# Attention with two feed-forward layers on one core: the first eight pairs' scores in plain float32 from four landing buffers, PSUM banks held back until a result has room, five buffers for the last outputs

## The chip, the cores and the metric

One NeuronCore of a Trainium2 chip runs the whole program. The metric is device time in microseconds (us) of one execution, lower is better. Five engines work side by side: PE (matrix multiply), DVE (VectorE), ACT (ScalarE), POOL (GpSimd) and SP, which here only issues DMAs.

## The reference

```python
# q, k, v: 4 batches, 8 heads, 576 positions, 64 wide (float32)
scores = scale * np.matmul(q, k.transpose(0, 1, 3, 2))
mask = block_i >= block_j          # blocks of 64 positions
scores = np.where(mask, scores, -1000000000.0)
scores = scores - np.max(scores, axis=-1, keepdims=True)
attn = np.exp(scores)
attn = attn / (np.sum(attn, axis=-1, keepdims=True) + 1e-09)
x = np.matmul(attn, v)             # laid out as 2304 tokens x 512
h = x @ w_in                       # 512 x 1024, softmax-like gate, layer norm with gain g_ln
y = ln @ w_out                     # 1024 x 512
h = y @ w_in2                      # 512 x 2048
out = (h / (1 + np.exp(-1.702 * h))) @ w_out2
```

## The kernel before

**Precision by terms.** A float32 operand is kept as two parts: H, a copy rounded to the type float32r (`qkH`, made by `nc.copy`), and L, the rest (`qkL = x - H`, made by `rest`, line 550). A product is then three matmuls: H with H, H with L, L with H. The probabilities times v (`u_pv`, line 671) are plain float32 matmuls instead, with no splitting; the trace shows each such instruction as two records.

**Pairs.** The 32 heads are worked in 16 pairs of two heads, four pairs to a batch. The two heads lie on partitions 0 to 63 and 64 to 127, so a score matmul of one head uses 64 rows of the array. A pair has an X part (queries 0 to 255: `scores(p, 0)`, `u_pt(p, "X")`, `u_pv(p, "X")`) and a Y part (the other 320 queries: `scores(p, 2)`, `scores(p, 3)`, `scores(p, "R")`, then `u_pt` and `u_pv`). R is the last block of 64 queries of both heads: before, `qR` holds them on the diagonal of a 128x128 tile, so that one matmul of 128 rows serves both heads.

**From scores to output.** `scores` (line 695) writes two PSUM banks; a reduction on DVE adds the mask, writes the result to an SBUF tile `P` and finds the row extreme `mx`; an exponential on ACT rewrites `P` and sums it into `sm`. `u_pt` (line 632) transposes `P` on PE into a bank, and ACT or DVE copies that to `ptx` or `pty`. `u_pv` multiplies by v; the result goes through `xo` to the DRAM tensor `xd`. There are two sets of `P` tiles (p % 2), one `pty` and one `ptx`. `norm` (line 748) ends a half of a batch: reciprocal of the sums `sm`, a transpose on PE (`ident,sm`), `rt` to DRAM. These eight transposes are good landmarks in the trace.

**Loads.** q and k of a pair land in the one buffer `raw_qk` (line 517). `load_qk` (line 602) takes column ranges, `split_qk` (line 619) makes H, L and the `qR` tiles: per pair one copy of 2x576 columns, one subtraction, four copies of 64x64. The X parts of pairs 0 to 3 come first, each from half of `raw_qk`; then the rest of q and k is loaded and split (for pairs 0 and 1 all of k a second time).

**Feed-forward layers.** `w1_prep` (line 586) turns the eight-byte weights of the first layer into float32 and splits them (tiles `e`, `r`, `w1i`, `w1o`). The first layer works on tiles of 128 tokens: `x_take`, `h_mm` (matmuls `w1i,xs`), `solu_ln`, `ln_t`, `y_mm`. The second layer runs after attention is over, its results go through the two buffers `ob` (list `obs`, line 1266) to the output (`out_steps`, line 1211).

**What sets the order.** All this is recorded by a `Recorder` (line 60) with a priority each, `a_time` for attention and `f_time` for the first layer (lines 979 to 1007: `T0` and `F_RATE` set when first-layer work is due, `PREP` when weight preparation is). `issue` (line 349) then writes one fixed program per engine: it takes the work with the earliest modelled start. Banks are handed out there: a group of matmuls that needs a bank gets one as soon as one is free. `_end` (line 336) chooses among engines for a copy and counts the waiting work of an engine up to `SPAN` behind in priority. On the chip each engine runs its list in order and waits on semaphores.

Of the kernel before, what the change touches and what calls it, by code (L numbers as in the profile page):

```python
# [21 lines left out]
def full(t):  # L22
    return t.bitcast(F32)
# [36 lines left out]
class Recorder:  # L60
# [6 lines left out]
    SPAN = 3  # L67
# [4 lines left out]
    def __init__(self, tc, banks):  # L72
        self.banks = banks
        self.n_bank = banks.shape[1]
        self.bank_free = [True] * self.n_bank
        self.bank_t = [0.0] * self.n_bank
        self.n_buf = 0
        self.places = {}

        self.floor = 0.0  # L80
        self.tc = tc
        self.nc = tc.nc
        self.prio = 0.0
        self.tag = None
        self.n_tag = {}
        self.open = None
        self.ops = []
        self.tensors = {}
        self.free = dict.fromkeys(self.ENGINES, 0.0)
        self.port = 0.0  # L90
        self.dma = 0.0
        self.now = 0.0
        self.heap = {e: [] for e in self.ENGINES}
        self.log = []
        for e in self.ENGINES:
            setattr(self, e, _Engine(self, e))
# [114 lines left out]
    def _cost(self, eng, name, kw, outs, ins):  # L211
# [5 lines left out]
        if eng == "tensor":  # L217
            if name == "transpose":
                return 0.109, 0.2, False
            k = kw["lhsT"].shape[0]  # L220
            if kw["lhsT"].dtype == F32:

                return max(0.109, 0.87 * n / 1000), 0.3, False
# [34 lines left out]
    def _add(self, forms):  # L258
# [10 lines left out]
        for eng, calls in forms.items():  # L269
            cost, port, lag = 0.0, False, 0.0  # L270
            for name, args, kw in calls:
# [12 lines left out]
                touched = [(self._place(a), False) for a in ins] + [(self._place(a), True) for a in outs]  # L284
# [137 lines left out]
def kernel(  # L422
# [22 lines left out]
    BLK = 64  # L445
# [21 lines left out]
    y1d = [dram.tile([DM, CH], F32, name=f"y1d{c}") for c in range(NC)]  # L467
    nc = Recorder(tc, psum.tile([128, 8, 512], F32, name="PS"))
# [48 lines left out]
    raw_qk = ap1.tile([128, 2, S], F32, name="rawqk")  # L517
# [84 lines left out]
    def load_qk(p, qs, ks, at):  # L602

        b, i = divmod(p, NPB)
        for n, (x, s) in enumerate(((q, qs), (k, ks))):
            nc.sync.dma_start(out=raw_qk[:, n, s.start + at:s.stop + at], in_=x[b, i, :, s])
# [12 lines left out]
    def split_qk(p, qs, ks, at):  # L619

        for i, s in ((slice(0, 2), qs),) if qs == ks else ((0, qs), (1, ks)):
            H, L = (x[:, i, s] for x in qkb[p % 2])
            r = raw_qk[:, i, s.start + at:s.stop + at]
            nc.copy(H, r)
            rest(L, r, H)
        if qs.stop == S:
            for t, r in zip(qkb[p % 2], qR[p % 2]):
                for h in range(2):
                    d = slice(64 * h, 64 * h + 64)
                    nc.copy(r[d, d], full(t)[d, 0, S - BLK:S])  # L630

    def u_pt(p, what):
# [8 lines left out]
        if two:  # L641
            t2 = nc.bank(1, 2, name="T")
        for blocks, h, i in todo:
            n = len(blocks)
            t = t2[:, h] if two else nc.bank(1, name="T")
# [3 lines left out]
            src = t[:, 0:n * 128]  # L649
            if two:  # L650
                if h == 0:
                    continue
                src = t2[:, :, 0:n * 128]
                h = slice(0, 2)
            pty = ptyb[p % NPTY]
            if what == "R":
                if i:
                    dst = pty[:, :, 3 * NQ:3 * NQ + BLK]
                    src = src.rearrange("p (h s) -> p h s", h=2)
                else:  # L660
                    dst = pty.rearrange("p h (j s) -> p h j s", s=NQ)[:, :, :, QX:NQ]
                    src = src.rearrange("p (j h s) -> p h j s", j=n, h=2)
            elif what == "X":
                dst = ptx[:, h]
            else:
                at = slice(128 * (i - 2), 128 * (i - 1))
                dst = pty.rearrange("p h (j s) -> p h j s", s=NQ)[:, h, 0:i + 1, at]
                src = src.rearrange("p h (j s) -> p h j s" if two else "p (j s) -> p j s", s=128)
            nc.copy(dst, src, "av")
# [25 lines left out]
    def scores(p, what):  # L695
# [5 lines left out]
        (qH, kH), (qL, kL) = ((x[:, 0], x[:, 1]) for x in qkb[p % 2])  # L701
        t = [nc.bank(2, name="S") for _ in range(2)]
        if what == "R":
            H, L = qR[p % 2]
            half = S // 2
            for c in range(2):
                ks = slice(c * half, (c + 1) * half)
                with nc.group():
                    for n, (x, y) in enumerate(((H, kH), (H, kL), (L, kH))):
                        nc.tensor.matmul(t[c][:, 0:half], lhsT=x, rhs=y[:, ks], start=n == 0, stop=n == 2)  # L710
# [6 lines left out]
        else:  # L717
# [3 lines left out]
            with nc.group():  # L721
                for i in ((0, 1) if what == 0 else (what,)):
                    w = 128 * (i + 1)
                    for n, (x, y) in enumerate(((qH, kH), (qH, kL), (qL, kH))):
                        for h in range(2):
# [3 lines left out]
                                start=n == 0, stop=n == 2,  # L729
# [136 lines left out]
    def attention():  # L866
# [20 lines left out]
        def load(p, qs, ks, vt, half=0):  # L887
            yield 0.0, (load_qk, p, qs, ks, QX * half)
            yield 0.0, (load_v, p, vt)

        def split_1(p, qs, ks, vt, half=0):
            yield 0.0, (split_qk, p, qs, ks, QX * half)


        todo = [(p, first, first, vx, p % 2) for p in range(NPB)]
        for p in range(2):
            yield from load(*todo[p])
        yield 0.0, (clear,)
        yield from split_1(*todo[0])
        for p in range(NPB):  # L900
            if p + 1 < NPB:
                yield from split_1(*todo[p + 1])
            if p + 2 < NPB:
                yield from load(*todo[p + 2])
            yield from x_part(p)
        yield 0.0, (norm, 0, 0)
        yield 0.0, (ended, QX)
        turn = list(range(NPB - 2, NPB)) + list(range(NPB - 2))
        todo = [(p, later, later if p >= NPB - 2 else every, vy) for p in turn]
        todo += [(p, every, every, ve) for p in range(NPB, NP)]  # L910

        def take(*a):
            yield from load(*a)
            yield from split_1(*a)

        yield from take(*todo[0])
        yield from take(*todo[1])
        for n, (p, *_) in enumerate(todo):
            both = [(y_part(p, take(*todo[n + 2]) if n + 2 < len(todo) else None), 7.5)]
            if n + 1 < len(todo) and todo[n + 1][0] >= NPB:  # L920
                both.append((x_part(todo[n + 1][0]), 2.0))
# [57 lines left out]
    T0 = 5  # L979
# [3 lines left out]
    F_RATE = 1.6  # L983
    PREP = 3
# [226 lines left out]
    def out_steps(cc, p):  # L1211
# [12 lines left out]
        for i, a in enumerate(acc[cc]):  # L1224
# [5 lines left out]
            if last:  # L1230
                a.buf.held = False
                o = obs[next(n_ob) % len(obs)]
# [119 lines left out]
```

## Time and profile before

| | us |
|---|---|
| median of 3 runs | 798.61 |
| lowest and highest | 798.06, 798.86 |
| profiled execution | 797.17 |
| its span, first to last instruction | 795.4 |

The profiled execution lies 1.44 us under the median, and its span 1.77 us under its own time. In the views a row of the timeline gives start, duration, engine, line, operation and out<-in with the partition and element counts; "x4" is four instructions merged into a row; in brackets stands the idle time before and the instruction that ended it. The ends of matmuls are modelled and overlap with the next start, so a step on PE is best priced from its start to the start of what follows. Almost every instruction carries line 347, where the recorder emits.

### The profile page before, as it was taken

How to read it: one execution, taken by the hardware profiler on the slowest of the kernel's cores; microseconds unless marked ns; L12 is line 12 of the kernel's file. 1: busy time of each engine (PE TensorE's matmuls, PEld its weight loads, DVE VectorE, ACT ScalarE, POOL GpSimd, SP SyncE). 2: the span in 40 equal slices, each digit the busy share in tenths (PEclk: the TensorE clock that was granted, in tenths of full speed). 3: DMA queues.
4: the chain of work that ended last, by engine and by line, in shares of the span. 5: the costliest groups of instructions: out<-in, count | busy, mean ns of one | idle time of the engine just before them, and what ended most of it. 6: DMA issues, size and time to landing. Idle time of an engine off the chain costs nothing.

```text
span 795.4 us, 14078 instructions
## 1 busy us (share of the span) xinstructions
PE 765.7 (96%) x4984; PEld 659.5 (83%) x4984; DVE 555.6 (70%) x1256; ACT 455.7 (57%) x1034; POOL 292.6 (37%) x355
## 2 busy tenths in 40 slices
PE   5898999999999999999999999999999999999996
PEld 3576777888787899898998789898988898989895
DVE  3689877655766487855747987978899765565643
ACT  5798978675856565645634645445575543434431
POOL 2245642361430254632322514324632342353310
PEclk9999999999999999999999999999999999999999
DMA  7654734533421254366411163644525222050201
GB/s 194 201 153 147 224 111 129 155 104 108 124 70 59 93 144 158 108 192 192 144 57 53 55 202 103 190 166 147 187 70 183 79 97 89 28 160 1 68 13 53
DMA packets 82342, 95.63 MB, mean 120 GB/s; under 512 B 11232, under 2 KB 57696, under 8 KB 82272
## 3 DMA queue, kind: packets, MB, share of 16 engines
q1 hardware_dynamic: 82272, 94.74, 38.2%
q8 instruction: 39, 0.64, 0.3%
q14 instruction: 31, 0.25, 0.1%
HBM read 69.47 MB, written 25.24 MB: 119 GB/s over the span
## 4 chain that ended last, share of the span: by engine, by line
PE 80%; DVE 9%; ACT 3%; DMA 3%; issue 2%; POOL 1%; SPq 1%; DVEq 0%; ACTq 0%; POOLq 0%
PE PS L347 80%; DMA e<-in_moe_w_in_dram 1%; SPq L347 1%; DVE sg L347 1%; DVE gL L347 1%; DVE w2oL L347 1%; ACT pty L347 1%; DVE w2SL L347 1%; DVE hc L347 1%; DVE u L347 1%; DVE w1i L347 1%; DVE e L347 1%; DVE qkL L347 1%; DVE st L347 1%; DMA r<-rcd 0%
## 5 line engine op out<-in xcount | busy, mean ns | idle before, releaser
L347 ACT ACTIVATE sg<-hc 128x256 f32<-128x256 f32 (+1 forms) x128 | 56.3, 443 | 108.3 <-DVE hc L347 99.5
L347 PE MATMUL PS<-w2oH,gH 128*128 128x512 f32 x288 | 113.4, 394 | 0.4 <-ACT gH L347 0.4
L347 PE MATMUL PS<-w2oH,gL 128*128 128x512 f32 x288 | 113.5, 394 | 0.2 <-DVE gL L347 0.2
L347 PE MATMUL PS<-w2oL,gH 128*128 128x512 f32 x288 | 113.4, 394 | 0.0
L347 PE MATMUL PS<-lnTH,w1o 128*128 128x256 f32 x576 | 111.2, 285 | 0.0
L347 PE MATMUL PS<-w1i,xs 128*128 128x512 f32 x432 | 108.0, 397 | 0.8 <-ACT pty L347 0.8
L347 PE MATMUL PS<-w1i,w2SH 128*128 128x320 f32 (+1 forms) x512 | 105.7, 296 | 0.2
L347 PEld LDWEIGHTS PS<-lnTH,w1o 128*128 128x128 f32 x576 | 91.1, 188 | 1.6 <-issue 0.6
L347 PEld LDWEIGHTS PS<-w1i,xs 128*128 128x128 f32 x432 | 78.2, 188 | 16.3 <-ACT pty L347 1.0
L347 PEld LDWEIGHTS PS<-w1i,w2SH 128*128 128x128 f32 x512 | 84.4, 189 | 5.0 <-DVE w1i L347 0.5
L347 POOL TENSOR_TENSOR sg<-hc,sg 128x256 f32<-128x256 f32 (+1 forms) x45 | 36.7, 817 | 128.0 <-ACT sg L347 124.1
L347 PE MATMUL PS<-lnTL,w1o 128*128 128x256 f32 x288 | 81.3, 282 | 0.0
L347 ACT ACTIVATE gH<-sg 128x256 fp32r<-128x256 f32 (+1 forms) x122 | 53.1, 442 | 44.2 <-DVE sg L347 29.0
L347 PE MATMUL PS<-w1i,w2SL 128*128 128x320 f32 (+1 forms) x256 | 75.6, 295 | 0.0
L347 ACT ACTIVATE P<-P,mx 128x128 f32<-128x128 f32 (+3 forms) x128 | 70.6, 554 | 7.5 <-DVE mx L347 7.2
L347 DVE CUSTOM_DVE_ANT_0 P<-PS,mask 128x128 f32<-128x128 f32 (+3 forms) x128 | 57.3, 486 | 22.2 <-PE PS L347 18.9
L347 DVE TENSOR_TENSOR hc<-PS,u 128x320 f32<-128x320 f32 (+1 forms) x96 | 42.8, 454 | 40.4 <-PE PS L347 37.4
L347 PEld LDWEIGHTS PS<-w2oH,gL 128*128 128x128 f32 x288 | 54.0, 188 | 13.5 <-DVE gL L347 1.2
L347 PEld LDWEIGHTS PS<-w2oH,gH 128*128 128x128 f32 x288 | 54.1, 188 | 10.3 <-ACT gH L347 1.2
L347 PEld LDWEIGHTS PS<-w2oL,gH 128*128 128x128 f32 x288 | 54.1, 188 | 8.9
L347 DVE TENSOR_TENSOR gL<-sg,gH 128x320 fp32r<-128x320 f32 (+1 forms) x95 | 48.1, 517 | 10.9 <-ACT gH L347 10.1
L347 PEld LDWEIGHTS PS<-lnTL,w1o 128*128 128x128 f32 x288 | 54.3, 189 | 0.7 <-DVE lnTL L347 0.2
(164 smaller groups left out, 1731.6 us busy)
## 6 DMA issues: line engine op xcount, KB each, us to landing
land<-in_moe_w_in_dram SPq DMA_DIRECT2D x16, 512.0 KB, 4.1
land<-in_moe_w_out_dram SPq DMA_DIRECT2D x16, 512.0 KB, 4.2
x<-y1d SPq DMA_DIRECT2D x16, 512.0 KB, 3.8
w2d<-wt SPq DMA_DIRECT2D x24, 256.0 KB, 2.6
wt<-w2d SPq DMA_DIRECT2D x24, 256.0 KB, 2.6
y1d<-yo SPq DMA_DIRECT2D x36, 128.0 KB, 1.7
part<-ob SPq DMA_DIRECT2D x18, 256.0 KB, 3.5
out_dram<-ob SPq DMA_DIRECT2D x18, 256.0 KB, 2.5
```

What stands on the lines that cost most here:

```text
L347: getattr(getattr(self.nc, e), name)(*map(real, args), **{k: real(v) for k, v in kw.items()})
```

## The change

- **Landing buffers.** Three buffers `rawqk0` to `rawqk2` and a piece of `x_all` take the place of the one `raw_qk`; pairs use them in turn as they use the v buffers. q and k of a pair come whole, or for pairs 0 to 3 as first 256 and later 320 columns, nothing twice.
- **Plain float32 scores.** For pairs 0 to 7 (`NFULL`) there is no H, no L and no `qR`: one float32 matmul from the landing buffer takes the place of three. R becomes, per half of the keys, one matmul of 64 rows to 64 partitions for each head, both heads into one bank. Pairs 8 to 15 stay as they were.
- **Banks.** With `also` the destination that the result of a bank will be copied to counts as written by the matmul group itself, so the group, and its bank, waits until that destination is free.
- **First activation.** An exponential on one column (`begun`) is issued at the start.
- **Last outputs.** In the last pass over the last chunk the three tiles `t` join the two `ob`.
- **Numbers.** SPAN 3 to 10, T0 5 to 10, F_RATE 1.6 to 1.4, PREP 3 to 2, and a lag for plain float32 matmuls of 64 rows.

```diff
-    SPAN = 3
+    SPAN = 10
...
-                touched = [(self._place(a), False) for a in ins] + [(self._place(a), True) for a in outs]
+                touched = [(self._place(a), False) for a in ins] + [(self._place(a), True) for a in outs + self.also]
+                self.also = []
...
+    begun = const.tile([128, 1], F32, name="begun")
+    tc.nc.scalar.activation(out=begun, in_=mhalf, func=ACTF.Exp)
...
-    raw_qk = ap1.tile([128, 2, S], F32, name="rawqk")
+    rawb = [ap1.tile([128, 2, S], F32, name=f"rawqk{i}") for i in range(3)]
+    rawb.append(x_all[:, 1024:1024 + 2 * S].rearrange("p (n s) -> p n s", n=2))
+
+    NFULL = 8
...
+    def split_qk(p):
+
+        if p < NFULL:
+            return
+        H, L = qkb[p % 2]
+        r = rawb[vat(p)]
+        nc.copy(H, r)
+        rest(L, r, H)
...
+            if not two or h == 0:
+                nc.also = [dst]
...
+        if p < NFULL:
+            terms = [(rawb[vat(p)][:, 0], rawb[vat(p)][:, 1])]
+        else:
+            (qH, kH), (qL, kL) = ((x[:, 0], x[:, 1]) for x in qkb[p % 2])
+            terms = [(qH, kH), (qH, kL), (qL, kH)]
         t = [nc.bank(2, name="S") for _ in range(2)]
+
+        nc.also = [P[x] for x in (["R"] if what == "R" else [(h, i) for h in range(2) for i in ((0, 1) if what == 0 else (what,))])]
...
+            with nc.group():
+                for c in range(2):
+                    ks = slice(c * half, (c + 1) * half)
+                    for h in range(2) if p < NFULL else ():
+                        d = slice(64 * h, 64 * h + 64)
+                        x, y = terms[0]
+                        nc.tensor.matmul(
+                            t[c][d, 0:half], lhsT=x[d, S - BLK:S], rhs=y[d, ks], start=True, stop=True
+                        )
...
-                    for n, (x, y) in enumerate(((qH, kH), (qH, kL), (qL, kH))):
+                    for n, (x, y) in enumerate(terms):
...
         for p in range(NPB):
+            yield from load(p, first, vx)
+            if p == 0:
+                yield 0.0, (clear,)
+        for p in range(NPB):
             yield from x_part(p)
+            yield from load(p, later, vy)
...
-    T0 = 5
+    T0 = 10
...
-    F_RATE = 1.6
-    PREP = 3
+    F_RATE = 1.4
+    PREP = 2
...
-                o = obs[next(n_ob) % len(obs)]
+
+                at = obs + [x[:, 0:DM] for x in tmpb] if p == NPAIR - 1 and cc == len(chunks) - 1 else obs
+                o = at[next(n_ob) % len(at)]
```

On PE, from pair 1's transposes to the end of pair 2's first scores, the list before stands so (`P` and `ptx` as above, `v` the values, `ident` marks a transpose, numbers are buffers):

```order
L347 MATMUL PS<-ident,P_155 128x128
L347 MATMUL PS<-ident,P_157 128x128 x2
L347 MATMUL PS<-ident,P_156 128x128
L347 MATMUL PS<-ident,P_158 128x128 x2
L347 MATMUL PS<-ptx,v_140 64x256 x2
L347 MATMUL PS<-ptx,v_140 64x128 x2
L347 MATMUL PS<-qkH_135 128x128 x2
L347 MATMUL PS<-qkL_136,qkH_135 128x128 x2
L347 MATMUL PS<-qkH_135,qkL_136 128x128 x2
L347 MATMUL PS<-qkH_135 128x256 x2
L347 MATMUL PS<-qkL_136,qkH_135 128x256 x2
L347 MATMUL PS<-qkH_135,qkL_136 128x256 x2
```

and with the change, from the very first matmul:

```order
L350 MATMUL PS<-rawqk_136 128x128 x2
L350 MATMUL PS<-rawqk_136 128x256 x2
L350 MATMUL PS<-rawqk_137 128x128 x2
L350 MATMUL PS<-rawqk_137 128x256 x2
L350 MATMUL PS<-ident,P_151 128x128
L350 MATMUL PS<-ident,P_153 128x128 x2
L350 MATMUL PS<-ident,P_152 128x128
L350 MATMUL PS<-ident,P_154 128x128 x2
L350 MATMUL PS<-rawqk_138 128x128 x2
L350 MATMUL PS<-rawqk_138 128x256 x2
L350 MATMUL PS<-ptx,v_143 64x256 x2
L350 MATMUL PS<-ptx,v_143 64x128 x2
```

Two rows of scores stand where six stood, and pair 2's scores (`rawqk_138`) come right behind pair 0's transposes, ahead of pair 0's product with v; before, pair 2's (`qkH_135`) came behind pair 1's product (`v_140`).

On SP, the loads at the start, before (`e` are first-layer weights):

```order
L347 DMA v_140<-in_v_dram 128x2x128
L347 DMA v_141<-in_v_dram 128x2x128
L347 DMA v_142<-in_v_dram 128x2x128
L347 DMA e_119<-in_moe_w_in_dram 128x1024
L347 DMA e_121<-in_moe_w_in_dram 128x1024
L347 DMA e_120<-in_moe_w_in_dram 128x1024
L347 DMA v_141<-in_v_dram 128x2x128
L347 DMA v_141<-in_v_dram 64x128
L347 DMA rawqk<-in_q_dram 128x256
L347 DMA rawqk<-in_k_dram 128x256
```

and with the change:

```order
L350 DMA v_144<-in_v_dram 128x2x128
L350 DMA rawqk_138<-in_q_dram 128x256
L350 DMA rawqk_138<-in_k_dram 128x256
L350 DMA v_145<-in_v_dram 128x2x128
L350 DMA x<-in_q_dram 128x256
L350 DMA x<-in_k_dram 128x256
L350 DMA v_146<-in_v_dram 128x2x128
L350 DMA e_121<-in_moe_w_in_dram 128x1024
L350 DMA rawqk_136<-in_q_dram 128x320
L350 DMA rawqk_136<-in_k_dram 128x320
```

The q and k of pairs 2 and 3 (`rawqk_138` and `x`) now stand ahead of the weights instead of behind them.

On PE, the first first-layer matmuls, before, among pairs 2 and 3 of the Y parts (`qkH_137` is pair 3, `pty` the transposed probabilities):

```order
L347 MATMUL PS<-qkH_137,qRL_146 128x288
L347 MATMUL PS<-pty_166,v_141 64x320 x6
L347 MATMUL PS<-pty_166,v_141 64x192 x2
L347 MATMUL PS<-pty_166,v_141 64x64 x2
L347 MATMUL PS<-w1i,xs 128x512 x6
L347 MATMUL PS<-ident,P_159 128x128 x3
```

and with the change, behind the Y parts of the whole first batch and the second `norm`:

```order
L350 MATMUL PS<-ident,PR_167 128x128 x5
L350 MATMUL PS<-ptx,v_146 64x256 x2
L350 MATMUL PS<-ptx,v_146 64x128 x2
L350 MATMUL PS<-w1i,xs 128x512 x24
L350 MATMUL PS<-ident,P_155 128x128 x3
```

Between the first and the second `norm` the list before has 48 such matmuls, the new one none.

## Rows read from the trace of the kernel before

**Rows 1.** Page, part 1: busy time and share of the span by engine.
```profile
PE 765.7 (96%) x4984; PEld 659.5 (83%) x4984; DVE 555.6 (70%) x1256; ACT 455.7 (57%) x1034; POOL 292.6 (37%) x355
```
**Rows 2.** Busy time by stretch: stretch, length, busy us by engine, granted clock, DMA.
```profile
0.00:28.80 28.80, 16.89 (x96) 11.18 (x96) 14.52 (x50) 16.52 (x49) 7.06 (x23) 0.94 0.70 201
28.80:83.20 54.40, 49.95 (x348) 37.39 (x349) 44.46 (x123) 48.92 (x124) 27.27 (x39) 1.00 0.55 163
83.20:145.60 62.40, 59.25 (x447) 47.38 (x444) 47.39 (x119) 49.49 (x122) 26.47 (x34) 1.00 0.51 153
145.60:265.50 119.90, 119.90 (x968) 97.06 (x965) 73.83 (x234) 81.72 (x214) 38.02 (x49) 1.00 0.32 95
```
**Rows 3.** Timeline of the first 29 us, ACT and PE.
```profile
4.64 1.28 ACT L347 ACT_TABLE_LOAD   x1 [4.64 <-DMA rawqk<-in_k_dram]
...
6.61 0.47 PE L347 MATMUL PS<-qkH 64*128 64x128 f32 x2 [6.61 <-ACT qkH L347]
...
12.61 0.69 PE L347 MATMUL PS<-ident,P 128*128 128x128 f32 x2 [0.36 <-DMA e<-in_moe_w_in_dram]
...
15.35 1.12 PE L347 MATMUL PS<-ident,P 128*128 128x128 f32 x4
...
19.86 0.33 PE L347 MATMUL PS<-qkH 64*128 64x128 f32 x2 [0.99 <-ACT qkH L347]
...
28.83 0.28 PE L347 MATMUL PS<-ident,sm 128*16 128x128 f32 x1
```
**Rows 4.** Chain that ended last, first 20 us: start, us, what.
```profile
6.25 9.29 DMA e<-in_moe_w_in_dram
...
16.13 0.53 SPq L347
...
19.84 0.70 DVE qkL L347
```
**Rows 5.** Groups by shape on ACT and DVE, 0 to 146 us: splitting of q and k.
```profile
L347 ACT ACTIVATE qRH<-qkH 64x64 fp32r<-64x64 f32 x13 | 3.2, 250 | 0.3
...
L347 ACT ACTIVATE qkH<-rawqk 128x1152 fp32r<-128x1152 f32 x2 | 2.3, 1164 | 0.0
...
L347 DVE TENSOR_TENSOR qkL<-rawqk,qkH 128x1152 fp32r<-128x1152 f32 x5 | 6.8, 1358 | 0.0
```
**Rows 6.** Timeline of PE in three stretches: scores of a pair, products with v.
```profile
44.71 0.44 PE L347 MATMUL PS<-qkH 64*128 64x384 f32 x2
...
45.44 0.66 PE L347 MATMUL PS<-ident,P 128*128 128x128 f32 x4
46.02 0.50 PE L347 MATMUL PS<-qkH 64*128 64x512 f32 x2
...
46.91 0.66 PE L347 MATMUL PS<-ident,P 128*128 128x128 f32 x4
47.33 0.38 PE L347 MATMUL PS<-qkH,qRH 128*128 128x288 f32 x1
...
48.20 1.55 PE L347 MATMUL PS<-w1i,xs 128*128 128x512 f32 x6
...
62.14 0.33 PE L347 MATMUL PS<-qkH 64*128 64x128 f32 x2
...
63.03 0.77 PE L347 MATMUL PS<-ident,PR 128*128 128x128 f32 x5
...
84.69 0.87 PE L347 MATMUL PS<-ptx,v 128*64 128x256 f32 x8
85.49 0.77 PE L347 MATMUL PS<-ident,P 128*128 128x128 f32 x5
```
**Rows 7.** Timeline of DVE, the last output adds.
```profile
788.72 0.69 DVE L347 TENSOR_TENSOR ob<-PS,land 128x512 f32<-128x512 f32 x1 [0.67 <-PE PS L347]
790.19 0.69 DVE L347 TENSOR_TENSOR ob<-PS,wt 128x512 f32<-128x512 f32 x1 [0.78 <-DMA out_dram<-ob]
791.53 0.69 DVE L347 TENSOR_TENSOR ob<-PS,wt 128x512 f32<-128x512 f32 x1 [0.65 <-DMA out_dram<-ob]
```

More of the change, by code (lines that the diff above doesn't have):

```diff
@@ L283, in _add @@
                         a.buf.left += 1
[L284 removed]
+                touched = [(self._place(a), False) for a in ins] + [(self._place(a), True) for a in outs + self.also]
+                self.also = []
                 for place, write in touched:
@@ L600, in w1o_prep, with load_qk @@
         w1_prep(moe_w_out[j * 128:(j + 1) * 128, :], w1o[0][j], w1o[1][j], g_sb[:, j:j + 1])
-    def load_qk(p, qs, ks, at):
+    def load_qk(p, s):
         b, i = divmod(p, NPB)
-        for n, (x, s) in enumerate(((q, qs), (k, ks))):
-            nc.sync.dma_start(out=raw_qk[:, n, s.start + at:s.stop + at], in_=x[b, i, :, s])
+        for n, x in enumerate((q, k)):
+            nc.sync.dma_start(out=rawb[vat(p)][:, n, s], in_=x[b, i, :, s])
     def load_v(p, ts):
@@ L617, in load_v @@
             nc.sync.dma_start(out=t[0:64, KT - 1], in_=v[b, i, (KT - 1) * 128:S])
[L619 to L630, printed above, removed]
+    def split_qk(p):
[5 more added lines that the diff above has]
+        rest(L, r, H)
+        for t, r in zip(qkb[p % 2], qR[p % 2]):
+            for h in range(2):
+                d = slice(64 * h, 64 * h + 64)
+                nc.copy(r[d, d], full(t)[d, 0, S - BLK:S])
     def u_pt(p, what):
@@ L642, in u_pt @@
             t2 = nc.bank(1, 2, name="T")
+        pty = ptyb[p % NPTY]
         for blocks, h, i in todo:
             n = len(blocks)
+            hs = slice(0, 2) if two else h
+            if what == "R" and i:
+                dst = pty[:, :, 3 * NQ:3 * NQ + BLK]
+            elif what == "R":
+                dst = pty.rearrange("p h (j s) -> p h j s", s=NQ)[:, :, :, QX:NQ]
+            elif what == "X":
+                dst = ptx[:, hs]
+            else:
+                at = slice(128 * (i - 2), 128 * (i - 1))
+                dst = pty.rearrange("p h (j s) -> p h j s", s=NQ)[:, hs, 0:i + 1, at]
             t = t2[:, h] if two else nc.bank(1, name="T")
+            if not two or h == 0:
+                nc.also = [dst]
             with nc.group():
@@ L648, in u_pt @@
                     nc.tensor.transpose(t[:, m * 128:(m + 1) * 128], Pb[p % NPB_][x][:, j * 128:j * 128 + 128], ident)
[L649 to L667, printed above, removed]
+            if two and h == 0:
+                continue
+            src = t2[:, :, 0:n * 128] if two else t[:, 0:n * 128]
+            if what == "R" and i:
+                src = src.rearrange("p (h s) -> p h s", h=2)
+            elif what == "R":
+                src = src.rearrange("p (j h s) -> p h j s", j=n, h=2)
+            elif what != "X":
                 src = src.rearrange("p h (j s) -> p h j s" if two else "p (j s) -> p j s", s=128)
@@ L705, in scores @@
             half = S // 2
[L706 to L709, printed above, removed]
+            with nc.group():
+                for c in range(2):
+                    ks = slice(c * half, (c + 1) * half)
+                    for h in range(2) if p < NFULL else ():
+                        d = slice(64 * h, 64 * h + 64)
+                        x, y = terms[0]
+                        nc.tensor.matmul(
+                            t[c][d, 0:half], lhsT=x[d, S - BLK:S], rhs=y[d, ks], start=True, stop=True
+                        )
+                    for n, (x, y) in enumerate(((H, kH), (H, kL), (L, kH)) if p >= NFULL else ()):
                         nc.tensor.matmul(t[c][:, 0:half], lhsT=x, rhs=y[:, ks], start=n == 0, stop=n == 2)
@@ L728, in scores @@
                                 t[h][:, at:at + w], lhsT=x[d, 128 * i:128 * i + 128], rhs=y[d, 0:w],
-                                start=n == 0, stop=n == 2,
+                                start=n == 0, stop=n == len(terms) - 1,
                             )
@@ L885, in attention, with load, take @@
         vx, vy, ve = slice(0, QX // 128), slice(QX // 128, KT), slice(0, KT)
-        def load(p, qs, ks, vt, half=0):
-            yield 0.0, (load_qk, p, qs, ks, QX * half)
+        def load(p, s, vt):
+            yield 0.0, (load_qk, p, s)
             yield 0.0, (load_v, p, vt)
[L891 to L899, printed above, removed]
+        def take(p):
+            yield from load(p, every, ve)
+            yield 0.0, (split_qk, p)
         for p in range(NPB):
[L901 to L904, printed above, removed]
+            yield from load(p, first, vx)
+            if p == 0:
+                yield 0.0, (clear,)
+        for p in range(NPB):
             yield from x_part(p)
+            yield from load(p, later, vy)
         yield 0.0, (norm, 0, 0)
         yield 0.0, (ended, QX)
[L908 to L921, printed above, removed]
+        turn = list(range(NPB - 2, NPB)) + list(range(NPB - 2)) + list(range(NPB, NP))
+        for n, p in enumerate(turn):
+            nxt = turn[n + 2] if n + 2 < NP else 0
+            both = [(y_part(p, take(nxt) if nxt >= NPB else None), 7.5)]
+            if n + 1 < NP and turn[n + 1] >= NPB:
+                both.append((x_part(turn[n + 1]), 2.0))
             yield from merge(both)
```

4 lines of the change are left out of this document (2 added, 2 removed).

## Prediction

> **What bounds the kernel now.** The first view is the page's busy table: PE is busy 96% of the span, 765.7 us, the others far less [rows 1]. So the time is the work of PE plus what PE loses, and the question is where it loses. The second view, busy time by stretch, cut at the `norm` transposes, answers that. From 145.6 to 265.5 PE has no idle time. Ahead of that it lacks 28.8 - 16.9 = 11.9 us in the first stretch, 4.45 in the second and 3.15 in the third, 19.5 us together [rows 2]. Over the second and third stretch (116.8 us) ACT is busy 48.9 + 49.5 = 98.4 us and DVE 44.5 + 47.4 = 91.9: they run at 84 and 79% and hold PE back there. Once PE is full, whatever PE gained early arrives at the end whole, since the later work is the same.
>
> The third view is the timeline of the start. ACT loads its table at 4.64, only when the first k has landed, for 1.28 us; a copy follows, and the first matmul starts at 6.61. Pair 2's first matmul starts at 19.86, the first `norm` transpose at 28.83 [rows 3]. The chain of waits tells why pair 2 is late: it runs through the weight loads (9.29 us), then SP's issue of pair 2's load at 16.13, then the splitting [rows 4]. There is one landing buffer, and its next loads stand behind the weights on SP.
>
> The clock belongs here: four transposes took 1.12 us at 15.35 [rows 3], and 0.66 later [rows 6], which is about the ratio of the levels 1.2 and 2.4 GHz; PE had worked with gaps until then. The granted-clock column shows only a part of it, 0.94 for the stretch [rows 2].
>
> I read the change against the profiled execution, 797.17 us, and shift the result by the 1.44 us that it lies under the median.
>
> **The change part by part.**
>
> *Start to first norm.* The table load leaves the path, because the dummy activation needs no DMA, and so does the copy. The first matmul can start when q and k are there, about 4.7: 1.9 us earlier. The loads of pairs 2 and 3 are issued ahead of the weights. What pair 2 then waits for is its set of `P`, which pair 0's transposes free. Those stand at 12.61 now [rows 3]; 1.9 earlier, and without the split of pair 1 between, I put pair 2 at about 12, instead of 19.86. From there to the transpose it takes 28.83 - 19.86 = 9.0 us now; with two splits fewer I take 8.5. That makes 20.5 for the first `norm` instead of 28.8: **-8.3 us**. Bounds: ACT is busy 16.5 us in this stretch [rows 2]; without the table load (1.28) and four copies of 512 columns (0.6 each, an estimate by columns from the 1.16 for 1152 in [rows 5]) some 12.8 stay, so 4.7 + 12.8 = 17.5 is the least (-11.3). At most, PE stays at the low clock all along: a pair takes there about twice its 0.89 of scores, 0.80 of products and six transposes at 0.11 [rows 6], 4.7 us, four pairs 19, and with the round trips between some 21 from 4.7 on: 26 (-2.8). That is also about where late loads would put it.
>
> *Splitting.* A pair loses a copy of 1152 columns (1.16 us), a subtraction (1.36) and four small copies at 0.25 [rows 5]: 3.5 us of ACT, DVE or POOL, 28 us over eight pairs. About 5 of that lie ahead of the first `norm` and are counted there. Of the other 23 some two thirds, 15, lie on ACT and DVE, 7.7 each, which at 84% busy is at most 9 us of stretch. But PE has just 4.45 + 3.15 = 7.6 us of shown idle time there, and part of that is round trips PE-DVE-ACT that stay. I take half the bound, **-4 us**, bounds -9 and 0. The rule on banks and the new numbers of the order act on the same idle time; I cost them at nothing beside this. What hides a group's later start is other work ready on PE; if that is gone, it is the third rival.
>
> *PE work.* Three float32r matmuls give way to one plain float32. The trace has the prices, start to start [rows 6]. Before: the X scores 63.03 - 62.14 = 0.89, the 384-column step 45.44 - 44.71 = 0.73, the 512-column step 0.89, R 48.20 - 47.33 = 0.87. The nearest plain float32 row is `ptx,v`: two heads, 256 + 128 columns each, 85.49 - 84.69 = 0.80. Those heads use two halves of the array's columns, the new scores two halves of its rows; I take the same price for it. So X costs 0.80, the 384 step 0.80, the 512 step 0.80 x 512/384 = 1.07 (less its fixed part, 1.01), R with 2 x 288 = 576 columns 1.2 (likewise 1.12). The difference per pair is -0.09 + 0.07 + 0.12 + 0.25 = 0.35, over eight pairs **+2.8 us**. Bounds 0 (the first four X parts run in idle time) and +6 (0.1 more at each of 32 groups).
>
> *Tail.* The third last add waits for an output DMA, the fourth too, and starts at 791.53; the second starts at 788.72 [rows 7]. With five buffers they follow at 0.69 each: the fourth would start at 790.10, 1.4 us earlier. The four DMAs then crowd, so I take **-1.0**, bounds -1.4 and 0.
>
> Sum: -8.3 - 4 + 2.8 - 1.0 = -10.5. The profiled execution comes to 786.7, the median to **788.1**. All bounds together reach from -22 to +3.
>
> **The rivals.**
>
> *Rows of the array do not work abreast in plain float32.* The trace shows six float32r matmuls of 64 rows and 384 columns in 0.73 us [rows 6], which at one column per cycle of 2.4 GHz (0.16 us each) one after another would be 0.96, so they do go abreast. In plain float32 only halves of the columns are shown to. If the halves of rows don't, the eight pairs' 8 x 1856 columns at 0.80/384 us are spent twice: +31 us, of which PE's remaining idle time takes perhaps 8. Then 788.1 + 31 - 8 = 811, slower.
>
> *Only R goes one head after the other.* Both heads' R results go to one bank, by different halves of the rows; no row before does that. It costs R's 576 columns once more per pair, 1.1 us, 8.8 for eight: 796.9. The Trainium skill says so (page "TensorEngine Tiling (Array Packing)", section Restrictions and Gotchas): different row tiles cannot access the same PSUM bank at the same time. By that rule the sum would be this rival's; no trace here bears it out yet, and since the two heads write different partitions of the bank, I give it little.
>
> *The filler is missing, and the end is later than before.* Between the first and the second `norm` the list before has 48 first-layer matmuls in it, the new list none. At 0.23 to 0.26 us each (six take 1.55 with the last one's modelled end [rows 6]) they are about 11 us that fill PE while ACT and DVE work. If attention alone keeps the stretch near its 54.4 us [rows 2], these 11 us come on top at the end, and the gain of 4 goes: 788.1 + 4 + 11 = 803. The point from which it decides is 54.4 - 11 = 43 us for the new stretch; the four pairs' own work on ACT is less than that, 48.9 less the splits and most of the weight preparation, which speaks against.
>
> *Early work stays late.* If the loads of four pairs at once crowd the DMA engines (70% busy in the first stretch already [rows 2]), or the low clock lasts, the first term is -2.8, the second near 0, and with +2.8 and -1.0 the median is 797.6, no change that can be told.
>
> **How the numbers follow.** Forecast 0.66, first rival 0.06, second 0.08, third 0.12, fourth 0.08. A measurement of this kernel can tell some 0.2%, 1.6 us, from no change, so faster means under 797.0. The forecast is faster nearly always; half of the second rival and a third of the fourth add to it: 0.74. Slower than 800.2 takes the first and nearly all of the third: 0.17. Within: 0.09. The forecast's own range from its bounds is 781 to 796; the range that leaves out the first rival and the ends goes on to 804, past the third rival.
>
> **What would show it.** Right: the table load ahead of 2 us, the first matmul near 4.7, pair 2's scores near 12, the first `norm` transpose at 19 to 23; the second one under 58; the X score group at about 0.8 us and R at about 1.1; the last adds 0.7 apart. Wrong: score steps of twice that; R alone at 2.2; the second `norm` still more than 45 us behind the first with PE idle in between; pair 2 waiting for q and k. The forecast falls if PE's idle time before it becomes full doesn't shrink by some 10 us.

## The result, and the profile after

The changed kernel takes 785.87 us, the median of 5 runs (782.48 to 786.93), against 798.38 for the kernel before in 5 runs beside it (796.39 to 798.86): a ratio of 0.984 with a 95% interval of 0.982 to 0.986, some 12.5 us less. The profiled execution of the changed kernel is that of 785.87, with a span of 784.1, 11.3 under the span before.

The busy table, the counterpart of [rows 1]:

```profile
PE 763.0 (97%) x4936; PEld 651.8 (83%) x4936; DVE 526.0 (67%) x1196; ACT 449.2 (57%) x1022; POOL 308.0 (39%) x368
```

DVE lost 30 us of work, ACT 6.5, POOL gained 15. Busy time by stretch, cut at the first, second, third, fourth and eighth `norm` transpose (columns as in [rows 2]):

```profile
0.00:22.55 22.55, 14.77 (x88) 9.00 (x88) 10.06 (x43) 13.75 (x46) 4.82 (x20) 0.92 0.81 240
22.55:61.90 39.35, 37.56 (x241) 21.76 (x240) 27.39 (x89) 29.33 (x76) 9.48 (x11) 0.91 0.62 189
61.90:109.60 47.70, 46.75 (x323) 30.73 (x321) 34.98 (x101) 41.52 (x111) 23.76 (x27) 1.00 0.59 186
109.60:117.40 7.80, 6.57 (x61) 4.97 (x59) 6.62 (x28) 7.18 (x18) 5.53 (x8) 1.00 0.70 201
117.40:270.70 153.30, 153.05 (x1159) 127.69 (x1158) 88.73 (x260) 105.06 (x256) 51.45 (x68) 1.00 0.30 84
```

PE's idle time ahead of the full stretch is 7.78 + 1.79 + 0.95 + 1.23 = 11.75 us, where it was 19.5. The second `norm` comes 39 us after the first. The timeline of the start, ACT and PE, against [rows 3]:

```profile
0.72 1.28 ACT L473 ACT_TABLE_LOAD   x1 [0.72 <-PEq L1342]
...
4.75 3.31 PE L350 MATMUL PS<-rawqk 64*128 64x128 f32 x16 [4.75 <-DMA rawqk<-in_k_dram]
...
9.05 0.93 PE L350 MATMUL PS<-rawqk 64*128 64x128 f32 x8
9.91 0.87 PE L350 MATMUL PS<-ptx,v 128*64 128x256 f32 x8
...
17.05 0.63 ACT L350 ACTIVATE w1i<-r 128x512 fp32r<-128x512 f32 x1 [1.90 <-DVE r L350]
...
18.11 0.89 PE L350 MATMUL PS<-ptx,v 128*64 128x256 f32 x6 [2.26 <-ACT ptx L350]
18.93 1.77 PE L350 MATMUL PS<-ident,P 128*128 128x128 f32 x6
20.70 1.93 PE L350 MATMUL PS<-ptx,v 128*64 128x256 f32 x8
22.55 0.28 PE L350 MATMUL PS<-ident,sm 128*16 128x128 f32 x1
```

The first matmul starts at 4.75 and pair 2's first scores at 9.05. Then PE waits 2.26 us for a copy to `ptx`, which stands on ACT behind the rounding of first-layer weights (`w1i`, 17.05), which waits for DVE. Behind the wait the last pair's transposes and its product with v take 22.55 - 18.93 = 3.62 us; at the full clock they would be 6 x 0.11 + 0.80 = 1.46 [rows 6]. The granted clock is at its lower level here for a part of the time (last section), but that is the smaller part of the difference. The run with two last buffers (below) has the same list on PE, and in its profiled execution the same work took 21.79 - 18.96 = 2.83 us, with a granted clock of 1.00 from 15 to 25 us:

```profile
18.96 1.39 PE L350 MATMUL PS<-ident,P 128*128 128x128 f32 x6
20.50 1.35 PE L350 MATMUL PS<-ptx,v 128*64 128x256 f32 x8
21.79 0.28 PE L350 MATMUL PS<-ident,sm 128*16 128x128 f32 x1
```

So the clock makes some 0.8 us of it. Most of the rest is short waits: in the changed kernel PE's weight loads (PEld) waited four times for ACT in this stretch, 1.2 us together.

What PE waited for up to the fourth `norm`, in the view of waits (us in total, times, longest), before the change (0 to 146 us):

```profile
PE PS L347 <- ACT qkH L347: 7.6, 2, 6.6
PE PS L347 <- DVE qkL L347: 3.4, 5, 1.5
```

and after (0 to 120 us), where both are gone; the 4.8 us of the first row are the start itself, as 6.6 of the 7.6 were before:

```profile
PE PS L350 <- DMA rawqk<-in_k_dram: 4.8, 1, 4.8
PE PS L350 <- ACT ptx L350: 3.1, 2, 2.3
PE PS L350 <- DVE mx L350: 3.0, 3, 1.2
```

PE's prices, timeline, against [rows 6]:

```profile
12.12 0.93 PE L350 MATMUL PS<-x 64*128 64x128 f32 x8
12.97 0.87 PE L350 MATMUL PS<-ptx,v 128*64 128x256 f32 x8
...
56.58 0.92 PE L350 MATMUL PS<-rawqk 64*128 64x384 f32 x4
57.43 0.66 PE L350 MATMUL PS<-ident,PR 128*128 128x128 f32 x4
...
60.81 1.13 PE L350 MATMUL PS<-rawqk 64*128 64x512 f32 x4
61.87 0.28 PE L350 MATMUL PS<-ident,sm 128*20 128x128 f32 x1
...
64.28 1.19 PE L350 MATMUL PS<-rawqk 64*64 64x288 f32 x8
65.40 0.92 PE L350 MATMUL PS<-x 64*128 64x384 f32 x4
```

Start to start that is X 0.85, the 384 step 0.85, the 512 step 1.06, R 1.12: 3.88 us a pair, against 0.89 + 0.73 + 0.89 + 0.87 = 3.38 before. The last adds on DVE and the last matmul, against [rows 7]; `t` and `ob` are the output buffers:

```profile
776.24 0.69 DVE L350 TENSOR_TENSOR t<-PS,wt 128x512 f32<-128x512 f32 x1 [0.78 <-PE PS L350]
777.60 0.69 DVE L350 TENSOR_TENSOR ob<-PS,wt 128x512 f32<-128x512 f32 x1 [0.67 <-PE PS L350]
778.96 0.69 DVE L350 TENSOR_TENSOR t<-PS,land 128x512 f32<-128x512 f32 x1 [0.67 <-PE PS L350]
779.89 0.39 PE L350 MATMUL PS<-w2oH,gL 128*128 128x512 f32 x1
780.32 0.69 DVE L350 TENSOR_TENSOR t<-PS,land 128x512 f32<-128x512 f32 x1 [0.67 <-DMA out_dram<-ob]
```

Each add now follows the matmuls of its tile. From the start of the last matmul to the end it takes 4.2 us (779.89 to 784.08); before, 7.1 (788.30 to 795.39).

**An account of PE.** To compare kernels whose work stands in another order, I count every PE instruction ahead of a `norm` transpose at its price at the full clock: scores as above, a transpose 0.11, a first-layer matmul of 512 columns 0.23, and so on. The time of the transpose less this sum is what PE has lost by then: idle time, time at the lower clock and small overheads.

| lost by (us) | 1st norm | 2nd | 4th | 8th | last matmul | work counted | last matmul to end |
|---|---|---|---|---|---|---|---|
| before | 20.4 | 29.1 | 36.2 | 38.2 | 40.1 | 748.1 | 7.1 |
| changed | 13.5 | 20.7 | 26.1 | 27.9 | 27.7 | 752.2 | 4.2 |

The 11.3 us between the two spans are 12.4 of loss and 2.9 of tail, less 4.1 of added work (from rounded numbers). One execution differs from the next: two kernels below (two last buffers, no first activation) have the changed kernel's list on PE, and their fourth `norm` came at 115.2 and 115.5 instead of 117.4, their last matmul at 779.3 and 779.4 instead of 779.9. So a difference of 2 us by the fourth `norm`, or of 0.6 by the last matmul, says nothing yet. The figures of loss in some expectations below (42.0, 31.6, 38.1) were counted with lower prices for scores; by the account above they are 35.0, 26.1 and 27.9.

### The profile page after: what moved, and what is told of

It reads as the page before. It is cut to its first block, busy times and chain, and to the rows that moved or that the text cites. A ratio compares the mean times of both kernels' runs of the same rounds, so it can differ in the third digit from the quotient of the medians.

```text
span 784.1 us, 13949 instructions
## 1 busy us (share of the span) xinstructions
PE 763.0 (97%) x4936; PEld 651.8 (83%) x4936; DVE 526.0 (67%) x1196; ACT 449.2 (57%) x1022; POOL 308.0 (39%) x368
## 5 line engine op out<-in xcount | busy, mean ns | idle before, releaser
L350 PE MATMUL PS<-lnTH,w1o 128*128 128x256 f32 x576 | 108.8, 284 | 0.0
L350 POOL TENSOR_TENSOR sg<-hc,sg 128x320 f32<-128x320 f32 (+1 forms) x61 | 53.1, 873 | 125.6 <-ACT sg L350 123.2
L350 DVE TENSOR_TENSOR hc<-PS,u 128x320 f32<-128x320 f32 (+1 forms) x96 | 43.2, 455 | 55.6 <-PE PS L350 53.3
L350 ACT ACTIVATE gH<-sg 128x320 fp32r<-128x320 f32 (+1 forms) x120 | 52.2, 442 | 40.6 <-DVE sg L350 23.2
L350 DVE CUSTOM_DVE_ANT_0 P<-PS,mask 128x256 f32<-128x256 f32 (+3 forms) x128 | 57.3, 486 | 25.0 <-PE PS L350 23.8
L350 PEld LDWEIGHTS PS<-w2oH,gL 128*128 128x128 f32 x288 | 54.1, 188 | 12.5 <-DVE gL L350 0.8
L350 POOL TENSOR_TENSOR gL<-sg,gH 128x256 fp32r<-128x256 f32 (+1 forms) x49 | 43.4, 892 | 52.7 <-ACT gH L350 51.5
```

The costliest lines, as they stand in the source:

```text
L350: getattr(getattr(self.nc, e), name)(*map(real, args), **{k: real(v) for k, v in kw.items()})
```

## The experiments

Ratios are to the kernel before, run beside each, with 95% intervals; one thousandth is 0.8 us.

### The tail

With the change but two output buffers:

```diff
-                at = obs + [x[:, 0:DM] for x in tmpb] if p == NPAIR - 1 and cc == len(chunks) - 1 else obs
+                at = obs
```

> The changed kernel with two output buffers to the end, nothing else different on PE or ACT. The prediction's tail term: 1.0 us is given back, the span comes to about 785. Rival theory, from the two traces: with two buffers the adds are tied to the order of the tiles 0, 1, 2, 3 while PE finishes 2, 3, 0, 1, so the first add can't start before PE's third group of six is done; then the end of the span lies 7.1 us behind the start of PE's last matmul instead of 4.2, and 2.9 us are given back (median near 788.8). In the profile: four adds at 0, 1.36, 2.8 and 4.2 us, the first at PE's third group.

Ratio 0.987 (0.984 to 0.989), 788.03 us; from the last matmul to the end 7.15 us. And the kernel before, with the five buffers and nothing else of the change:

```diff
-                o = obs[next(n_ob) % len(obs)]
+                at = obs + [x[:, 0:DM] for x in tmpb] if p == NPAIR - 1 and cc == len(chunks) - 1 else obs
+                o = at[next(n_ob) % len(at)]
```

> The kernel before with nothing of the change but the five last output buffers. Until the last chunk its instructions are the same, and on PE the whole list is. Theory: two buffers in turn tie the last adds to the order of their tiles, although PE finishes the tiles in another order, and that costs what lies between the two tails: 7.1 us from the last matmul's start to the end before, 4.2 with the change. So 2.9 us less, 795.5 against 798.4 (ratio 0.996), and the tail at about 4.2 us. Rival, the prediction's term: only the waits for the output DMAs go, at most 1.4 us, with the first add still late: tail 5.7 to 6.1 us, 797.0 to 797.4.

Ratio 0.996 (0.995 to 0.998), 794.15 us, 3.0 less; tail 4.15. The timeline of its last adds, and the first of the four adds of the kernel before, which stands ahead of [rows 7]:

```profile
783.73 0.68 DVE L347 TENSOR_TENSOR t<-PS,wt 128x512 f32<-128x512 f32 x1
784.98 0.69 DVE L347 TENSOR_TENSOR ob<-PS,wt 128x512 f32<-128x512 f32 x1 [0.57 <-PE PS L347]
786.34 0.69 DVE L347 TENSOR_TENSOR t<-PS,land 128x512 f32<-128x512 f32 x1 [0.67 <-PE PS L347]
```

```profile
787.36 0.69 DVE L347 TENSOR_TENSOR ob<-PS,land 128x512 f32<-128x512 f32 x1 [1.63 <-PE PS L347]
```

With two buffers the adds come in the order `land`, `land`, `wt`, `wt`, while PE finishes the two tiles of `wt` first; so the first add stood waiting for PE's third tile. With five they come in PE's order. In both kernels it is the order of the adds, and not the waits for output DMAs alone, that makes the 2.9 us.

### Plain float32 or the rest

As changed, with no pair in plain float32; each part of q and k is split when it has landed:

```diff
-    NFULL = 8
+    NFULL = 0
...
+        yield 0.0, (split_qk, 0, first)
```

> The changed kernel with all sixteen pairs split into H and L again (three matmuls per score), but with the four landing buffers, the bank rule, the first activation, the new numbers and the five last buffers. My theory: the plain float32 saves 28 us of work on ACT, DVE and POOL ahead of the point where PE is full and costs PE some 0.5 us per pair (traced: 3.88 against 3.38), 4 in all; without it PE loses more early, some 8 us, and does 4 less: 3 to 5 us slower than the changed kernel, 789 to 791. Rival: the loads and the new order make the whole gain and the plain float32 only costs PE: then this is 4 us faster, near 782.

Ratio 1.000 (0.999 to 1.002), 799.25 us. Nothing is left of the gain, though the tail is short here too. Lost by the first `norm` 16.5 us, 3.9 less than before, so what is left of the change (buffers, order of the loads and the rest) does help the start; by the fourth 35.0, by the last matmul 43.2. What they won was lost again, and the plain scores are worth 43.2 - 27.7 = 15.5 us of loss for 4.1 of work. My theory had put that at some 8.

Four pairs, and all sixteen, in plain float32:

```diff
-    NFULL = 8
+    NFULL = 4
```

> As changed, but only the pairs 0 to 3 in plain float32, the pairs 4 to 7 split into parts as before. PE has some 4 x 0.5 = 2 us less to do. Theory: plain float32 pays wherever ACT and DVE hold PE back, and that is so until about 140 us, the Y parts of the second batch included, so half of the relief goes (without any plain float32 PE lost 42.0 us by the fourth norm, as changed 31.6): about 5 us more lost, 2 less worked, 788 to 790. Rival: the relief counts ahead of the second norm alone, and then the time is 784, since the loss stays and 2 us of work go.

Ratio 1.010 (1.008 to 1.011), 805.21 us: both theories missed, and by 15 us. By the second `norm` 22.6 us were lost, by the fourth 36.9, by the fifth 44.6. The trace led to the next question, below.

```diff
-    NFULL = 8
+    NFULL = 16
```

> As changed, but all 16 pairs in plain float32. PE has some 8 x 0.5 = 4 us more to do. Theory: from the fourth norm on PE is full, relief of ACT and DVE buys nothing there, so the 4 us come on top: 789 to 790. Rival: what PE still loses behind the fourth norm, 38.1 - 31.6 = 6.5 us, is also due to ACT and DVE, and goes: 784 to 786.

Ratio 0.987 (0.985 to 0.988), 786.39 us. The work is 4.1 more, the loss by the last matmul 26.5, 1.2 less. That lies between the two expectations; against the changed kernel's ratio the difference is 0.002, within the intervals. No gain from the last eight pairs is shown.

### Who holds DVE

In the kernel with four plain pairs the timeline shows, on DVE, POOL and PE:

```profile
114.89 2.79 POOL L350 TENSOR_TENSOR qkL<-x,qkH 128x1152 fp32r<-128x1152 f32 x1 [0.93 <-ACT qkH L350]
115.09 3.13 DVE L350 SCALAR_TENSOR_TENSOR e<-e 128x512 int32<-128x512 int32 x1
118.96 0.66 PE L350 MATMUL PS<-ident,e 128*128 128x128 f32 x4 [2.31 <-DVE mx L350]
...
136.38 1.47 POOL L350 TENSOR_SCALAR qkH<-rawqk 128x1152 fp32r<-128x1152 f32 x1 [2.06 <-PE PS L350]
136.76 1.63 DVE L350 SCALAR_TENSOR_TENSOR r<-r,e 128x512 int32<-128x512 int32 x1
139.00 1.17 PE L350 MATMUL PS<-qkH 64*128 64x512 f32 x2 [2.70 <-DVE mx L350]
```

A DVE step on weights, 0.69 us elsewhere, takes 3.13 and ends some 0.5 us after POOL's subtraction; behind it on DVE stand the reductions that PE waits for. In the same trace, by stretch, behind the two waits:

```profile
120.00:125.00 5.00, 5.00 (x27) 4.55 (x27) 4.53 (x13) 4.98 (x19) 1.96 (x3) 0.66 0.30 101
...
140.00:145.00 5.00, 5.00 (x24) 4.35 (x21) 3.14 (x5) 3.63 (x12) 2.02 (x3) 0.52 0.38 99
```

After each wait PE works on at a lower clock: full work, at 0.66 and 0.52 granted. So here a wait is paid twice. The edit that tests it ties the subtraction to DVE; first with four plain pairs:

```diff
-        rest(L, r, H)
+        nc.vector.tensor_tensor(out=L, in0=r, in1=full(H), op=ALU.subtract)
```

> The kernel with four pairs in plain float32, with one edit: the subtraction that makes the low part of q and k is tied to DVE, where the order had given five of twelve to POOL. Theory: a subtraction of 1152 columns on POOL (2.8 us) holds up any DVE instruction with two operands in SBUF until it ends: a step of 0.7 us took 3.13 at 115.1 us and 1.63 at 136.8, PE then waited 2.3 and 2.7 us on DVE and ran some 4 us each at half the clock. Without them these stalls are gone, and with them 2 x (2.5 + 2) = 9 us: 796. DVE takes 5 x 1.36 = 6.8 us more work, which costs some of that: 796 to 799, and no DVE step with two SBUF operands of 512 columns above 1.1 us beside a subtraction. Rival: the loss is DVE's and ACT's work as such, and the added 6.8 us of DVE make it 805 or more.

Ratio 0.990 (0.988 to 0.992), 791.15 us: 2.0% less than with POOL's share, better than expected. PE's waits for `mx` from 22 to 200 us, with POOL's share and without it (one row of each kernel):

```profile
PE PS L350 <- DVE mx L350: 9.2, 6, 2.7
```

```profile
PE PS L350 <- DVE mx L350: 3.1, 4, 1.4
```

and the weight step on DVE, groups by shape from 0 to 200 us, likewise:

```profile
L350 DVE SCALAR_TENSOR_TENSOR e<-e 128x512 int32<-128x512 int32 x16 | 14.7, 916 | 6.8 <-POOL e L350 6.8
```

```profile
L350 DVE SCALAR_TENSOR_TENSOR e<-e 128x512 int32<-128x512 int32 x16 | 11.9, 748 | 2.9 <-POOL e L350 2.8
```

One thing in the expectation was misread: the second hold (136.76) stands beside POOL's copy `qkH`, not a subtraction, and such copies stayed on POOL; beside one of them (38.85) a DVE step still took 1.65 us. The same edit in the changed kernel:

> As changed, with the subtraction of q and k (pairs 8 to 15) tied to DVE, where the order had given five of eight to POOL. Theory of the held DVE: as changed only one DVE step is held long (3.0 us instead of 0.7 at 75.4) and PE does not wait for it, so nothing to win: 785 to 787. Rival: holds too short to stand out add up, and the time falls below 784.

Ratio 0.980 (0.977 to 0.982), 783.02 us, against 0.984 (0.982 to 0.986): the intervals just touch. That is the rival's side, a gain of some 3 us. Lost by the fourth `norm` 22.9 us (26.1 as changed), by the last matmul 24.8 (27.7). And with no plain float32:

> The kernel with no plain float32 at all, with the subtraction of q and k tied to DVE, where POOL had ten of twenty. Theory of the held DVE: a good part of what plain float32 brought is that POOL no longer holds DVE; then this is well under the 799 of the same kernel with POOL's share: 793 to 796. Rival: plain float32 brings what it takes off DVE and ACT as work; then ten subtractions more on DVE (some 11 us, over 140 us that DVE is 75% busy) make it no better: 799 to 804.

Ratio 0.997 (0.995 to 0.998), 796.71 us: 3 us less, just above what the theory gave.

So POOL's subtractions cost in these three kernels (a fourth, at the end, shows nothing), and with them off POOL the ratio falls with the number of plain pairs: 0.997, 0.990, 0.980 for 0, 4 and 8. That the edit brings this is shown. That the hold is its only means is not: the order of all engines is written anew with each edit, and what single DVE instructions took above the usual for their kind, up to 160 us, fell only from some 8 to 5 us with four plain pairs.

### The start and the numbers

As changed, without the first activation:

```diff
-    tc.nc.scalar.activation(out=begun, in_=mhalf, func=ACTF.Exp)
```

> As changed, without the exponential on one column at the start; the table load then stands ahead of the first real exponential. Theory: since PE now starts with plain float32 straight from the landing buffer, no ACT work stands ahead of the first matmul any more, so the table is loaded while PE and DVE make the first scores, or holds up the first exponential by up to 1.3 us; the pairs behind wait for weights' work on ACT and DVE anyway, so 0 to 0.7 us more: 785.9 to 786.6. Rival: the table load stands whole on the path of the first pair and the 1.3 us arrive at the end: 787.2.

Ratio 0.983 (0.982 to 0.985), 783.87 us, no loss; the first `norm` is at 21.0. Theory and rival both missed: no run shows a gain from the first activation.

The four numbers as before:

```diff
-    SPAN = 10
+    SPAN = 3
...
-    T0 = 10
+    T0 = 5
...
-    F_RATE = 1.4
-    PREP = 2
+    F_RATE = 1.6
+    PREP = 3
```

> The changed kernel with SPAN 3, T0 5, F_RATE 1.6 and PREP 3 as before. My theory costs the numbers at nothing by themselves: within 2 us of the changed kernel (784 to 788). Rival: the numbers carry a good part of the gain, and without them it is 4 us or more slower (790 or more), with first-layer matmuls back between the first and the second norm.

Ratio 0.984 (0.981 to 0.986), 784.74 us, the same, as the theory had it. Yet the course differs: by the fourth `norm` only 17.2 us are lost, against 26.1, and by the last matmul 25.8 against 27.7. Seven of nine microseconds won early were given back; why isn't shown.

The weight preparation later:

```diff
+    LATE = 6
...
-        while prep and a_time > PREP * (17 - len(prep)):
-            nc.prio = PREP * (17 - len(prep))
+        while prep and a_time > LATE + PREP * (17 - len(prep)):
+            nc.prio = LATE + PREP * (17 - len(prep))
```

> The changed kernel with the preparation of the first layer's weights due 6 later in the recorder's priorities. In the trace of the changed kernel PE waits 2.3 us at 15.9 for a copy to ptx that stands behind a weight copy on ACT, and several us from 24 to 29 for reductions that stand behind weight steps on DVE, all of them behind a weight load that lands at 14.1; and PE's clock falls to its low level behind both gaps. If these waits are what is left of the start, moving the weights back closes them: the first norm at 20 instead of 22.6, less time at the low clock, and 3 to 6 us faster (780 to 783). Rival: the weights are then late for the first layer, PE idles there instead, and the time stays within 2 us or rises.

Ratio 0.988 (0.986 to 0.991), 789.34 us. Lost by the first and second `norm` 9.4 and 12.7 us, the best of all runs; by the last matmul 31.1. The rival's time came, but its cause isn't shown. Between the fourth `norm` and the fifth 7.4 us were lost, yet 96 first-layer matmuls stand there, as many as in the changed kernel between the same two. The two longest waits in that stretch, 1.53 us at 120.87 and 1.39 at 162.29, are for reductions that stand on DVE behind a small step on one column (`st`). That step took 2.23 and 2.43 us here, each beside a subtraction on POOL; in the changed kernel the same kind of step took 0.1 to 0.6 us up to 270 us. POOL, DVE and PE at the second:

```profile
159.23 2.65 POOL L350 TENSOR_TENSOR qkL<-rawqk,qkH 128x1152 fp32r<-128x1152 f32 x1
159.46 2.43 DVE L350 TENSOR_TENSOR st<-st 128x1 f32<-128x1 f32 x1
162.29 0.97 PE L350 MATMUL PS<-w1i,xs 128*128 128x512 f32 x3 [1.39 <-DVE mx L350]
```

So a part of this loss looks like that of the kernel with four plain pairs; the subtraction was not tied to DVE here, so how much stays open.

The two that did best or no worse, together (subtraction on DVE, numbers as before):

> As changed, with the subtraction of q and k tied to DVE and the four numbers of the order as before the change. Theory: the tie is worth 0.4% on its own and the numbers nothing that can be told, so this stands at a ratio of 0.977 to 0.982, 780 to 785 us, no different from the tie alone. Rival: the old numbers start first-layer work earlier, which left less of it to fill PE later in other runs; then what the tie wins is given back, 785 to 788.

Ratio 0.984 (0.982 to 0.986), 784.89 us: the time lies at the edge between the two, the ratio outside the theory's. On top of the old numbers the tie brought nothing that can be told. The lowest ratio is that of the changed kernel with the subtraction tied to DVE, 0.980; its interval reaches that of the kernel without the first activation.

The rule on banks wasn't tried by itself; what it costs or brings stays open.

## Why the prediction was right, and where its terms were off

The sum was -10.5 on the span, measured -11.3; the median 788.1, measured 785.87. That it is so near is in part luck: by the account the terms measured -6.9, -5.4, +4.1 and -2.9 against -8.3, -4, +2.8 and -1.0, each off by 1.3 to 1.9, and the errors cancel. What held is the mechanism: PE lost less ahead of the stretch where it is full, paid for with more PE work.

- **Start, -8.3.** The first `norm` came at 22.55, so -6.3, with one more product with v ahead of it (before, the fourth pair's stood behind the transpose); in loss it is -6.9. The table load, the first matmul and the order of the loads went as said; pair 2 came 3 us earlier than my 12. The step that failed is "from there to the transpose I take 8.5": it took 13.5. I priced that stretch by the old order. In the new list pair 2's scores stand ahead of all four products, so three more products and pair 1's transposes lie in it: 6.9 us of work instead of 3.9 by [rows 6] and the new X step. Of the other 6.6 us 2.26 are the wait for ACT and some 0.8 the lower clock behind it. My bound at 26 had the clock in it, but not this wait.
- **Splitting, -4.** From the first to the fourth `norm` PE lost 15.7 us before, 12.6 now, -3.1; behind it 3.9 and 1.6, another -2.3. I had put nothing behind the fourth, though with 2 us between executions where the gain fell is uncertain. The term's part in the whole was too small: without plain float32 all of the gain goes. I had booked two thirds of it on loads and table.
- **PE work, +2.8.** Measured 0.50 a pair, +4.0 (4.1 in the account). R was right at 1.12; the X and 384 steps cost 0.85 instead of the 0.80 of `ptx,v`, the 512 step 1.06 instead of 1.01. No row shows the "fixed part" that I took off there; by columns alone it is 1.07.
- **Tail, -1.0.** Measured -2.9, outside its bounds. I saw only the waits for output DMAs in [rows 7], not that the adds stood in another order than PE's tiles. So they came 1.36 us apart, each behind its tile, and not the 0.7 that I gave as a sign.
- **"Whatever PE gained early arrives at the end whole"** was wrong as a rule: it held for this change, but with the old numbers, with later weights and with no plain float32 most of the early gain was given back.
- **The signs.** Three more came out otherwise than I said: pair 2's scores at 9.05, not near 12; the second `norm` at 61.9, not under 58; and PE's idle time before it is full shrank by 7.8 us, not by some 10. By that last sign the forecast should have fallen. It didn't, since the tail gave more and since idle time is only a part of the loss, which shrank by 10.1 us up to the fourth `norm`.
- **Row halves not abreast: refuted.** Score steps at 0.85 and 1.06, not twice that.
- **Only R one head after the other: refuted.** Both heads' R, 2 x 288 columns, takes 1.12 us, my price for heads abreast; 2.2 was the rival's. The page "TensorEngine Tiling (Array Packing)" of the Trainium skill, section Restrictions and Gotchas, says that row tiles cannot access one bank at the same time; for two heads writing different partitions of a bank this trace differs, and the measurement decides.
- **Filler missing between the first two norms:** 39 us lie between them, under the 43 from which it would decide. In the run with later weights it isn't shown to have decided either.
- **Early work stays late:** no; the start kept 6 of 8 us.

## What to carry to other kernels

A cheaper form of work pays where the engines that prepare it hold the bottleneck: here 0.5 us more PE work a pair bought some 2 us of PE's lost time a pair in the first half, and next to nothing in the second, where PE was full. Before you count an early gain as kept, look at what the bottleneck waits for later; with a planned order each edit writes the whole program anew, so take the sum of lost time at several landmarks, not the first one alone, and see how far the same list scatters between executions. At a tail, compare the order in which results are made with the order in which they are drained.

## What was not expected of the hardware

**POOL can stop DVE for the length of an instruction.** The step of 0.69 us took 3.13 beside a subtraction of 2.79 on POOL; the changed kernel has one such place too, 3.0 us at 75.4. The Trainium skill states it (page "SBUF — State Buffer", section "SBUF: two separate sides"): DVE, with two inputs in SBUF, and GpSimd share a port pair; whichever starts first holds it for the whole instruction, and the other fully blocks. The trace at 115.09 agrees: POOL began at 114.89, and DVE's step ended only after POOL's.

**A wait can cost as much again in clock.** The changed kernel by stretch, behind its wait of 2.26 us:

```profile
15.00:20.00 5.00, 2.74 (x14) 1.50 (x14) 4.04 (x12) 2.90 (x11) 1.82 (x3) 0.88 0.91 292
20.00:25.00 5.00, 5.00 (x26) 2.54 (x25) 2.00 (x5) 2.34 (x5) 0.65 (x1) 0.78 0.93 291
25.00:30.00 5.00, 3.27 (x13) 1.52 (x10) 4.53 (x14) 3.15 (x8) 2.90 (x4) 0.91 0.67 190
30.00:35.00 5.00, 5.00 (x18) 2.30 (x16) 2.46 (x10) 0.79 (x4) 0.00 (x0) 0.50 0.51 173
```

PE was idle for 2.26 us, then for 0.84 and 0.89 (before 26.49 and 28.29), and behind the first and the last of these the granted clock fell once it worked again: 0.78 over 20 to 25 us, and 0.50, which is 1.2 GHz throughout, over 30 to 35. With the same list on PE, the run with two last buffers waited 0.95 us where this one waited 2.26, and its clock stayed at 1.00 from 15 to 25 us. The column doesn't show everything: from 0 to 9 us it says 1.00, yet the X scores of pairs 0 and 1 took 3.2 us (4.75 to 7.99) instead of 2 x 0.85.

With four plain pairs the mean over the span was 0.983, with the subtraction off POOL 0.995. As an estimate, 0.012 of 800 us is some 10 of the 18 us between these two spans (806.9 and 788.9). But the first is the slowest of its five executions; by the medians of all, 0.987 and 0.994, it is some 6 of 14 us.
